# Windowed attention and a feed-forward layer on one core: joining 64-bit weights on VectorE alone, and taking the second chunk's masks and transposes off TensorE

## The chip, the core and the metric

The kernel runs on one core of one Trainium2 chip. The metric is the device time of one launch in microseconds; the median of three runs of the kernel before is 801.97 us (801.61 to 802.2). Engines are named as in the profile: PE is TensorE, DVE is VectorE, ACT is ScalarE, POOL is GpSimd, and SP issues every DMA.

## The reference

```python
def _attn_ref(q, k, v):                       # (8, 8, 576, 64)
    scores = scale * np.matmul(q, k.transpose(0, 1, 3, 2))
    rel = pos[:, None] - pos[None, :]
    mask_plain = (rel >= 0) & (rel < window)                                   # window 32, heads 0 to 3
    mask_dil = (rel >= 0) & (rel < window * dilation) & (rel % dilation == 0)  # dilation 4, heads 4 to 7
    ...
    return np.matmul(attn, v)

def _moe_ref(x, w_in, w_out):                 # x (4608, 512), w_in (512, 2048), w_out (2048, 512)
    h = x @ w_in
    g = 0.5 * h * (1.0 + erf(h * inv_sqrt2))
    return (g @ w_out).astype(np.float32)
```

The attention output, heads side by side, is the `x` of the feed-forward layer. `w_in` and `w_out` arrive as 64-bit floats.

## The kernel before, in words

The 4608 tokens are cut into nine chunks: chunk `c` for `c` below 8 holds the first 512 positions of batch `c`, chunk 8 the last 64 positions of all batches. Chunk 0 goes through the feed-forward layer alone, while the weights are still coming in. The other eight go in four pairs of chunks (`two_chunks`), with a scheme of seven products in place of eight.

All dense products are made of float32r matmuls. Every operand is held as two parts, a rounded high part and the remainder, and a product is three matmuls: high by high, low by high, high by low. Each is one 128x128 weight against 512 columns; there are 3120 of them in the program. L565 is the first layer of chunk 0 (`h_part`, 192 matmuls), L585 its second layer (`ffn_o`, 192), L1108 the first layer of chunks 1 and 2 (384), L1181 and L1296 the layers of the rest.

**Weights.** One of 16 tiles holds 128 columns of `w_in` and 128 rows of `w_out`, 1 MB in 64 bits. `w_load` fetches it as pairs of 32-bit words. Then `w_mid` on ACT shifts the words by 16 bits, `w_split` on DVE takes five steps to build a float32 cut to the high part's bits and the exact remainder, and `w_high` copies the high part as float32r. The first four tiles are done in halves (`HALVED`). `w_away` writes the parts of a tile to a scratch tensor in DRAM, from where later stages fetch them.

**Attention.** A pair `s` is two heads of one chunk; a chunk has four. `scores` makes 32 blocks of 32 queries by 64 keys on PE. For chunks 0 and 1 the mask comes from PE too: two matmuls of 128x256 (L358) put it into PSUM ahead of the scores, which accumulate on it. `lowest` takes row maxima on DVE, `softmax` runs eight exponentials per pair on ACT, `inverse` and `norm` divide. For chunks 0 and 1 `turn_pe` transposes the probabilities on PE (four matmuls per pair, L491) and copies them out of PSUM into `zeros`, a tile in which every second block of 32 columns stays zero, so that `av_early` can contract over all 128 rows at once (16 matmuls per pair, L509). For chunks 2 to 7 the mask is applied by DVE as it reads the scores, `turn` transposes in 32x32 blocks on DVE, `move` lets ACT carry four blocks to other rows (L484), and `av` contracts over 64 rows (32 matmuls per pair, L530 in chunk 2). `xout` leaves `x`, in two parts.

**Order.** Up to the end of chunk 0 the order on every engine is written out by hand: `ORDER` is a string of words that is walked once, and each word runs the next step of one job on one engine. A letter names the job (q, Q, R load queries and keys of chunks 0, 1, 2; v, V values; d loads a weight; k, w, j are `w_mid`, `w_split`, `w_high`; s scores, l lowest, e softmax, i inverse, n norm, t turn, a the product with values, x `xout`, capitals for chunk 1, @ for chunk 2; h, g, o are the first layer, the GELU and the second layer; z is `w_away`), the letter after the colon the engine (p PE, a ACT, v DVE, d DMA). A word such as `*511` puts 11 matmuls of 128x512 without use into PSUM bank 5; there are 25 such matmuls. After that a planner (`Flow`) orders the rest from costs and due times; `duos` holds the times at which it wants the attention of chunks 2 to 8.

Of the kernel before, what the change touches and what calls it, by code (L numbers as in the profile page):

```python
# [39 lines left out]
ORDER = ("q0:d s0:p l0:v d0:d k0:a q1:d *36 s1:p w0:v l0:v w0:v w0:v d1:d k0:a q2:d q3:d w0:v e0:a e0:a j0:a k1:a v1:d w0:v "  # L40
# [111 lines left out]
def attn_ffn(ctx: ExitStack, tc: tile.TileContext, qk, qk_lp, qk_ld, v, v_ld, w, outT):  # L152
# [53 lines left out]
    zeros = wpool.tile([P, 2, 2, 2, 4, 2, KB], F32, tag="w", name="zeros")  # L206
    nc.gpsimd.memset(zeros, 0.0)
# [44 lines left out]
    def w_split(f):  # L252
        for cols in halves(f):
            mid, top, t = raws[f][:, cols, 0], raws[f][:, cols, 1], spare[:, cols]
            yield
            nc.vector.tensor_scalar(t, top, 3, 0x3FFFF000, op0=ALU.logical_shift_left, op1=ALU.bitwise_and)
            yield
            nc.vector.tensor_scalar(mid, mid, 0x01FFFFFF, None, op0=ALU.bitwise_and)
            yield
            nc.vector.scalar_tensor_tensor(top, top, 0xC0000000, t, op0=ALU.bitwise_and, op1=ALU.bitwise_or)  # L260
            yield
            nc.vector.tensor_scalar(t, top, 0xFF800000, None, op0=ALU.bitwise_and)
            yield
            nc.vector.scalar_tensor_tensor(part_of(f, 1, cols), tiled(mid), 2.0 ** -36, tiled(t.bitcast(F32)), op0=ALU.mult, op1=ALU.mult)

    def w_high(f):
        for cols in halves(f):
            e = yield
            copy(e, part_of(f, 0, cols), tiled(raws[f][:, cols, 1].bitcast(F32)))
# [57 lines left out]
    def load_v(s):  # L327

        yield {"DMA": 2.53}
        t = wpool.tile([P, 2, NU, 2, 2 * D], F32, tag="w", name="v_sb")  # L330
        nc.sync.dma_start(t, v[s.c, s.p // 2])
        for i in range(2):
            o = xs[s.c][s.p + i]
            o.v = t[:, i] if s.c > 1 else t[:, i].rearrange("p u j d -> p (u j) d").rearrange("p (a r) d -> p a r d", a=2)
# [10 lines left out]
    def slot(s, u):  # L345
        if s.c < 2:
            return u % 2 * 2 + u // 2
        return u if s.plain or s.rest else (u - 1) % NU

    def scores(s, bank):  # L350
# [5 lines left out]
        if s.c < 2:  # L356
# [4 lines left out]
        for u in range(NU):  # L361
            for r in range(4):
# [6 lines left out]
                for h in range(2):  # L369
# [3 lines left out]
                                     x[:, k0:k0 + s.nk], start=s.c > 1, stop=s.c > 1 or u == NU - 1)  # L373

    def lowest(s):
# [8 lines left out]
        if s.c < 2:  # L384
# [35 lines left out]
    def softmax(s):  # L420
# [6 lines left out]
        for i in range(2 * NU):  # L427
            if i % 4 == 0 and s.c == 0 or i == 0 or s.c > 1:
                yield {"ACT/exp": 1.2 if s.c == 0 else 2.4}
            t = s.sm[i // NU][:, i % NU]  # L430
            at = s.at + i % NU * 2 * KB
            nc.scalar.activation(t, s.sc[:, i // NU, at:at + 2 * KB] if s.c < 2 else t, AF.Exp, bias=s.st[:, 0, i:i + 1],  # L432
                                 scale=SCALE if s.c < 2 else -1.0, accum_out=s.st[:, 1, i:i + 1])
# [52 lines left out]
    def turn_pe(s):  # L486

        yield
        bank = s.bank + (s.p % 2 if s.c else 0)
        for i in range(NU):  # L490
            nc.tensor.transpose(ps[:, bank, i * P:(i + 1) * P], s.all[:, 2 * i:2 * i + 2].rearrange("p i k -> p (i k)"),  # L491
                                diag.bitcast(F32))
        s.t = zeros[:, s.p % 2]
        for k in range(2):
            e = yield
            rows = slice(64 * k, 64 * k + 64)
            copy(e, s.t[rows].rearrange("p h a r k q -> p (h a) r k q")[:, :, :, k],
                 ps[rows, bank].rearrange("p (i r q) -> p i r q", r=4, q=KB))

    def av_early(s):  # L500

        yield
        bank = s.bank + (s.p % 2 if s.c else 1)
        s.px = ps[:, bank]
        x = s.px.rearrange("p (r k a q) -> p a r k q" if s.plain else "p (k a q r) -> p a r k q", k=2, a=2, r=4)
# [953 lines left out]
```

## Time and profile before

| | |
|---|---|
| median of 3 runs | 801.97 us |
| lowest, highest | 801.61, 802.2 us |
| span of the profiled execution | 801.2 us |
| PE busy | 791.7 us (99%) |
| DVE busy | 652.2 us (81%) |
| ACT busy | 532.3 us (66%) |
| DMA moved | 214.62 MB, 268 GB/s on average |

The profiled execution is not one of the three timed runs, so what lies around its span is known from the median alone: 801.97 - 801.2 = 0.8 us. The share of busy time is an average over stages. PE's busy time covers pipelined matmuls whose ends are modelled, so that the distance between the starts of two blocks, and not the busy time, tells what a block costs. The chain of waits (the chain that ended last) shows which engine held the end back at each moment.

### The profile page before, as it was taken

Reading aid. Unit: us, or ns where it says so; the run is one execution under the profiler, and the core shown is the slowest. Engines: PE = TensorE matmul, PEld = TensorE weight load, DVE = VectorE, ACT = ScalarE, POOL = GpSimd, SP = SyncE. Lnnn points to the kernel's source line nnn. Section 1 sums busy time; section 2 is a strip of 40 time slices with the busy share of each in tenths; the row PEclk is TensorE's granted clock in tenths of the full one; section 3 lists DMA queues with packets and bytes.
Section 4 is the critical chain, followed back from the end, with each engine's and each line's share of the span. In section 5 each row is a group of like instructions: output and inputs, shape, how many; then the busy total and the mean of one; then the engine's idle time right before and its main releaser. Section 6 shows DMA issues by size and latency. Waiting matters only on the chain.

```text
span 801.2 us, 19134 instructions
## 1 busy us (share of the span) xinstructions
PE 791.7 (99%) x7806; PEld 650.6 (81%) x7806; DVE 652.2 (81%) x1081; ACT 532.3 (66%) x1294; POOL 39.2 (5%) x63
## 2 busy tenths in 40 slices
PE   7999999999999999999999999999999999999998
PEld 5888888888888878888888888888888888888886
DVE  7999989998999989778897688778986753589753
ACT  8998869678896467786654479775744534565441
POOL 6000033310000000000000000000000000000000
PEclk9999999999999999999999999999999999999999
DMA  9999974999987989674864489558654399555002
GB/s 371 417 415 392 395 272 140 337 353 398 412 307 260 367 317 353 261 301 134 347 244 157 159 317 380 200 210 321 232 211 158 120 388 366 181 205 198 12 1 105
DMA packets 53384, 214.62 MB, mean 268 GB/s; under 512 B 4913, under 2 KB 5425, under 8 KB 36273
## 3 DMA queue, kind: packets, MB, share of 16 engines
q1 hardware_dynamic: 53296, 213.40, 70.3%
q8 instruction: 61, 1.00, 0.5%
q14 instruction: 27, 0.21, 0.1%
HBM read 167.51 MB, written 42.99 MB: 263 GB/s over the span
## 4 chain that ended last, share of the span: by engine, by line
PE 95%; ACT 2%; DMA 1%; DVE 1%; SPq 0%; issue 0%; DVEq 0%; ACTq 0%
PE ps L1296 36%; PE ps L1181 29%; PE ps L1108 11%; PE ps L565 6%; PE ps L585 5%; PE ps L372 3%; PE ps L544 2%; DMA raw_qk<-qk 1%; PE ps L509 1%; ACT sm L432 1%; DVE parts L1039 1%; PE ps L491 1%; PE ps L522 1%; PE ps L530 0%; PE ps L647 0%; ACT turned L484 0%
## 5 line engine op out<-in xcount | busy, mean ns | idle before, releaser
L1296 PE MATMUL ps<-parts,ring 128*128 128x512 f32 x1344 | 308.2, 390 | 0.1
L1296 PEld LDWEIGHTS ps<-parts,ring 128*128 128x128 f32 x1344 | 251.4, 188 | 53.5 <-ACT u L171 0.5
L1181 PE MATMUL ps<-parts,ring 128*128 128x512 f32 x1008 | 232.7, 391 | 0.0
L1181 PEld LDWEIGHTS ps<-parts,ring 128*128 128x128 f32 x1008 | 188.3, 188 | 40.2
L1032 ACT CAST parts<-c 128x512 fp32r<-128x512 f32 x224 | 135.3, 620 | 94.8 <-DVE parts L1039 46.7
L1039 DVE TENSOR_TENSOR parts<-c,parts 128x512 fp32r<-128x512 f32 x224 | 151.7, 687 | 44.5 <-ACT parts L1032 42.4
L1215 DVE TENSOR_TENSOR c<-c 128x512 f32<-128x512 f32 x128 | 84.9, 685 | 0.0
L1165 ACT ACTIVATE c<-c 128x512 f32<-128x512 f32 x96 | 58.9, 629 | 33.8 <-DVE c L1158 30.1
L432 ACT ACTIVATE sm<-sm,st 128x64 f32<-128x64 f32 (+1 forms) x224 | 75.5, 339 | 4.6 <-DVE st L418 4.4
L173 DVE COPY c<-ps 128x512 f32<-128x512 f32 x60 | 41.4, 691 | 41.1 <-PE ps L1181 40.6
L1158 DVE TENSOR_TENSOR c<-c,ps 128x512 f32<-128x512 f32 x72 | 49.3, 686 | 16.2 <-PE ps L1181 13.4
L171 ACT COPY c<-ps 128x512 f32<-128x512 f32 x44 | 25.7, 588 | 41.0 <-PE ps L1181 38.4
L565 PE MATMUL ps<-x,weight 128*128 128x512 f32 x192 | 46.9, 394 | 0.0
L484 ACT COPY turned<-half 32x256 f32<-32x256 f32 x104 | 42.0, 404 | 6.1 <-DVE turned L474 3.5
L585 PE MATMUL ps<-g,weight 128*128 128x512 f32 x192 | 45.7, 390 | 0.0
L1108 PE MATMUL ps<-x,weight 128*128 128x512 f32 x192 | 45.4, 393 | 0.0
L1108 PE MATMUL ps<-x,ring 128*128 128x512 f32 x192 | 44.9, 392 | 0.0
L432 ACT ACTIVATION_READ_ACCUMULATOR sm<-sm,st 128x1 f32 x224 | 42.1, 188 | 0.0
L1108 PEld LDWEIGHTS ps<-x,ring 128*128 128x128 f32 x192 | 35.7, 188 | 7.7
L585 PEld LDWEIGHTS ps<-g,weight 128*128 128x128 f32 x192 | 35.9, 188 | 7.5
L1108 PEld LDWEIGHTS ps<-x,weight 128*128 128x128 f32 x192 | 35.6, 188 | 7.7
L565 PEld LDWEIGHTS ps<-x,weight 128*128 128x128 f32 x192 | 35.5, 188 | 7.6
(104 smaller groups left out, 778.3 us busy)
## 6 DMA issues: line engine op xcount, KB each, us to landing
ring<-sums SPq DMA_DIRECT2D x56, 1024.0 KB, 6.9
ring<-plain SPq DMA_DIRECT2D x46, 1024.0 KB, 8.4
v_sb<-v SPq DMA_DIRECT2D x17, 1024.0 KB, 12.0
raw_qk<-qk SPq DMA_DIRECT2D x32, 512.0 KB, 10.2
raw_w<-w SPq DMA_DIRECT2D x16, 1024.0 KB, 16.1
plain<-weight SPq DMA_DIRECT2D x32, 512.0 KB, 11.3
sums<-units SPq DMA_DIRECT2D x16, 1024.0 KB, 10.5
units<-plain SPq DMA_DIRECT2D x4, 1024.0 KB, 11.1
```

The lines of the kernel that those rows point to most:

```text
L432: nc.scalar.activation(t, s.sc[:, i // NU, at:at + 2 * KB] if s.c < 2 else t, AF.Exp, bias=s.st[:, 0, i:i + 1], scale=SCALE if s.c < 2 els ...
L484: nc.scalar.copy(s.t[32 * to:32 * to + 32, r % 2], s.half[32 * r:32 * r + 32])
L565: nc.tensor.matmul(bank, column(weights[f], t, cc), x[:, xx], start=n == 0, stop=n == 3 * NC - 1)
L585: nc.tensor.matmul(ps[:, d], column(weights[f], t, NC + d), gs[f][:, u], start=first and n == 0, stop=last and n == 2)
L1032: nc.scalar.copy(to if len(x.shape) == 2 else to.rearrange("p (g i) -> p g i", i=32), x)
L1039: nc.vector.tensor_sub(a, x, b)
L1108: nc.tensor.matmul(bank, column(w, i, cc), x[:, j], start=k == 0, stop=k == 3 * NC - 1)
L1158: nc.vector.tensor_add(C[f][:, part], C[f][:, part], ps[:, bank_of(bank)])
L1165: nc.scalar.activation(C[f][:, part], C[f][:, part], AF.Gelu)
L1181: nc.tensor.matmul(ps[:, bank_of(bank)], w()[:, a, i * P:(i + 1) * P], made[n, u, i][:, b], start=begins and k == 0, stop=k == 5, skip_gro ...
L1215: op(C[f][:, to], C[f][:, a], C[f][:, b])
L1296: nc.tensor.matmul(ps[:, bank_of((n, b, d))], w()[:, i, d * P:(d + 1) * P], made[key][:, j], start=begins and f == 0 and k == 0, stop=f == ...
```

## The change

`w_mid` and `w_split` go, and `w_whole` takes their place: three steps on DVE build a whole float32 from the two words. `w_high` copies it as float32r on ACT (or DVE) as before, and the new `w_low` subtracts that copy from it on DVE. In the attention of chunk 0 the tile with zero halves goes: `turn_pe` copies the four transposes out in one piece into `facing`, and `av_early` contracts over 64 rows, in twice as many matmuls of half the columns. Chunk 1 is treated as chunks 2 to 7 are: mask in DVE's pass, `turn` on DVE, `move` on ACT, `av` on PE. The first layer's first four tiles get four PSUM banks, so that all four can be under way at once. `ORDER` is written anew, with 12 matmuls without use instead of 25, and `duos` has new times.

```diff
-ORDER = ("q0:d s0:p l0:v d0:d k0:a q1:d *36 s1:p w0:v l0:v w0:v w0:v d1:d k0:a q2:d q3:d w0:v e0:a e0:a j0:a k1:a v1:d w0:v "
+ORDER = ("q0:d s0:p l0:v l0:v e0:a e0:a d0:d w0:v w0:v w0:v w0:v j0:a q1:d *25 s1:p l1:v l1:a e1:a e1:a w0:v i0:v k0:v i0:v "
...
-    zeros = wpool.tile([P, 2, 2, 2, 4, 2, KB], F32, tag="w", name="zeros")
-    nc.gpsimd.memset(zeros, 0.0)
+    facing = wpool.tile([P, NPAIR, 2, 2, 4, KB], F32, tag="w", name="facing")
...
-    def w_mid(f):
-
-        for cols in halves(f):
-            yield
-            raw = raws[f][:, cols].bitcast(U16).rearrange("p n t -> p (n t)").rearrange("p (n t) -> p n t", t=4)
-            nc.scalar.copy(raw[:, :, 0:2], raw[:, :, 1:3])
...
-    def w_split(f):
+    def w_whole(f):
         for cols in halves(f):
-            mid, top, t = raws[f][:, cols, 0], raws[f][:, cols, 1], spare[:, cols]
+            low, top, t = raws[f][:, cols, 0], raws[f][:, cols, 1], spare[:, cols]
             yield
-            nc.vector.tensor_scalar(t, top, 3, 0x3FFFF000, op0=ALU.logical_shift_left, op1=ALU.bitwise_and)
+            nc.vector.tensor_scalar(t, top, 3, 0x3FFFFFF8, op0=ALU.logical_shift_left, op1=ALU.bitwise_and)
             yield
-            nc.vector.tensor_scalar(mid, mid, 0x01FFFFFF, None, op0=ALU.bitwise_and)
+            nc.vector.scalar_tensor_tensor(t, low, 29, t, op0=ALU.logical_shift_right, op1=ALU.bitwise_or)
             yield
             nc.vector.scalar_tensor_tensor(top, top, 0xC0000000, t, op0=ALU.bitwise_and, op1=ALU.bitwise_or)
-            yield
-            nc.vector.tensor_scalar(t, top, 0xFF800000, None, op0=ALU.bitwise_and)
-            yield
-            nc.vector.scalar_tensor_tensor(part_of(f, 1, cols), tiled(mid), 2.0 ** -36, tiled(t.bitcast(F32)), op0=ALU.mult, op1=ALU.mult)
...
+    def w_low(f):
+        for cols in halves(f):
+            yield
+            nc.vector.tensor_sub(part_of(f, 1, cols), whole_of(f, cols), part_of(f, 0, cols))
...
     def scores(s, bank):
-        if s.c < 2:
+        if s.c == 0:
...
     def turn_pe(s):
-        s.t = zeros[:, s.p % 2]
-        for k in range(2):
-            e = yield
-            rows = slice(64 * k, 64 * k + 64)
-            copy(e, s.t[rows].rearrange("p h a r k q -> p (h a) r k q")[:, :, :, k],
-                 ps[rows, bank].rearrange("p (i r q) -> p i r q", r=4, q=KB))
+        s.t = facing[:, s.p]
+        e = yield
+        copy(e, s.t.rearrange("p h a r q -> p (h a r q)"), ps[:, s.bank])
...
     def av_early(s):
-                for h in range(2):
-                    nc.tensor.matmul(x[h * D:(h + 1) * D, a, r], s.v[:, a, r, h * D:(h + 1) * D],
-                                     s.t[:, h, a, r].rearrange("p k q -> p (k q)"), start=True, stop=True)
+                for k in range(2):
+                    rows = slice(64 * k, 64 * k + 64)
+                    for h in range(2):
+                        nc.tensor.matmul(x[h * D:(h + 1) * D, k, a, r], s.v[rows, a, r, h * D:(h + 1) * D],
+                                         s.t[rows, h, a, r], start=True, stop=True)
...
+    def hidden_bank(f):
+        return ps[:, (4, 5, 0, 1)[f] if f < 4 else 4 + f % 2]
...
-        return dict(l=lowest, e=softmax, i=inverse, n=norm, t=turn_pe, a=av_early)[kind](s)
+        return dict(l=lowest, e=softmax, i=inverse, n=norm, t=turn if s.c else turn_pe, m=moved, a=av_early)[kind](s)
...
-    duos = [(2, 0, 0.1, (0, 0), 9.8), (2, 2, 1.5, (3.0, 5.0), 15.9),
+    duos = [(2, 0, -5.9, (0.0, 0.0), 11.8),
+            (2, 2, -3.3, (0.2, 2.2), 13.1),
```

The functions `scores`, `lowest`, `softmax` and `xout` test `s.c == 0` where they tested `s.c < 2`, and the host lays out the values of chunk 1 as it does those of chunks 2 to 7.

How the instructions move, on PE at the start of the program. `early` holds the masks, `sm` the probabilities, `x,weight` is the first layer of chunk 0, `g,weight` its second layer. Before:

```order
L491 MATMUL ps<-early,sm 128x128 x4
L647 MATMUL ps<-early 128x512 x11
L491 MATMUL ps<-early,sm 128x128 x4
L509 MATMUL ps<-zeros,v_sb 64x2x32 x16
L647 MATMUL ps<-early 128x512 x2
L491 MATMUL ps<-early,sm 128x128 x4
L509 MATMUL ps<-zeros,v_sb 64x2x32 x16
L491 MATMUL ps<-early,sm 128x128 x4
L509 MATMUL ps<-zeros,v_sb 64x2x32 x16
L565 MATMUL ps<-x,weight 128x512 x6
L509 MATMUL ps<-zeros,v_sb 64x2x32 x16
L565 MATMUL ps<-x,weight 128x512 x18
```

The same place with the change:

```order
L486 MATMUL ps<-early,sm 128x128 x4
L653 MATMUL ps<-early 128x512 x7
L486 MATMUL ps<-early,sm 128x128 x4
L504 MATMUL ps<-facing,v_sb 64x32 x64
L564 MATMUL ps<-x,weight 128x512 x9
L486 MATMUL ps<-early,sm 128x128 x4
L564 MATMUL ps<-x,weight 128x512 x3
L486 MATMUL ps<-early,sm 128x128 x4
L504 MATMUL ps<-facing,v_sb 64x32 x64
L564 MATMUL ps<-x,weight 128x512 x36
```

Twelve matmuls of the first layer now stand ahead of the last two products with values, where six stood, and fewer matmuls without use stand between the transposes.

The same stretch on DVE with the change, from the first weight's remainder to the second pair's probabilities (L248, L250, L252 are `w_whole`, L265 `w_low`, L439 the reciprocal, L453 `norm`, L382 the row maxima):

```order
L265 TENSOR_TENSOR weight<-raw_w,weight 128x2x256
L439 RECIPROCAL st<-st 128x8
L382 TENSOR_REDUCE st<-ps 128x8
L453 TENSOR_TENSOR sm<-sm,st 128x512
L248 TENSOR_SCALAR spare<-raw_w 128x512
L250 SCALAR_TENSOR_TENSOR spare<-raw_w,spare 128x512
L252 SCALAR_TENSOR_TENSOR raw_w<-raw_w,spare 128x512
L248 TENSOR_SCALAR spare<-raw_w 128x512
L439 RECIPROCAL st<-st 128x8
L250 SCALAR_TENSOR_TENSOR spare<-raw_w,spare 128x512
L453 TENSOR_TENSOR sm<-sm,st 128x512
```

The second weight tile's first steps now stand ahead of the second pair's `norm`; that weight is the sixth transfer that SP issues, as the fourth pair's queries and keys were before.

ACT ahead of the second half of chunk 1's products with values (L571, L574 are the GELU and its rounding, L428 the exponentials, L480 `move`, L451 a `norm` on ACT, L550 `xout`):

```order
L480 COPY turned<-half 32x256 x4
L571 ACTIVATE gf<-ps 128x512
L451 ACTIVATE sm<-sm,st 128x64 x8
L574 CAST g<-gf 128x512
L571 ACTIVATE gf<-ps 128x512
L428 ACT_TABLE_LOAD
L428 ACTIVATE sm,st<-sm,st 128x64 x4
L480 COPY turned<-half 32x256 x4
L550 CAST x<-ps 128x512 x2
L428 ACTIVATE sm,st<-sm,st 128x64 x7
L574 CAST g<-gf 128x512
L571 ACT_TABLE_LOAD
L571 ACTIVATE gf<-ps 128x512
L480 COPY turned<-half 32x256 x4
```

The moves of chunk 1's blocks, which did not exist, stand in one queue with the GELUs of chunk 0 and the exponentials of chunk 2.

## Rows read from the trace of the kernel before

**Rows 1.** The page: busy time of PE and the other engines; shares of the chain.

```profile
PE 791.7 (99%) x7806; PEld 650.6 (81%) x7806; DVE 652.2 (81%) x1081; ACT 532.3 (66%) x1294; POOL 39.2 (5%) x63
...
PE 95%; ACT 2%; DMA 1%; DVE 1%; SPq 0%; issue 0%; DVEq 0%; ACTq 0%
```

**Rows 2.** Chain of waits, start and end: start us, us, what.

```profile
3.16 11.29 DMA raw_qk<-qk
...
25.14 1.58 PE ps L565 x6
26.72 1.08 PE ps L509 x32
27.80 4.30 PE ps L565 x18
...
797.41 0.02 issue
```

**Rows 3.** Chain of waits, pieces of chunk 1 and chunk 2 on PE.

```profile
32.11 0.23 PE ps L358 x2
32.34 0.79 PE ps L372 x53
...
34.35 2.95 PE ps L565 x12
37.30 2.72 PE ps L585 x12
...
61.79 0.87 PE ps L491 x8
...
65.40 2.02 PE ps L509 x64
...
129.30 1.41 PE ps L372 x91
130.71 8.41 PE ps L1108 x36
139.12 2.00 PE ps L530 x128
```

**Rows 4.** Groups on PE over the run, shapes apart: busy, mean ns | idle before.

```profile
L544 PE MATMUL ps<-v_sb,turned 64*32 64x64 f32 x1408 | 16.8, 225 | 0.1
```

**Rows 5.** Timeline of DVE, 21 to 24 us: start, duration, instruction.

```profile
21.68 0.20 DVE L443 RECIPROCAL st<-st 128x8 f32<-128x8 f32 x1
21.92 0.69 DVE L457 TENSOR_TENSOR sm<-sm,st 128x512 f32<-128x512 f32 x1
...
23.25 0.42 DVE L256 TENSOR_SCALAR spare<-raw_w 128x512 uint32<-128x512 uint32 x1
...
23.91 0.69 DVE L260 SCALAR_TENSOR_TENSOR raw_w<-raw_w,spare 128x512 uint32<-128x512 uint32 x1
```

**Rows 6.** Timeline of ACT: `xout` reading PSUM.

```profile
22.02 0.59 ACT L554 CAST x<-ps 128x512 fp32r<-128x512 f32 x1
```

**Rows 7.** Groups on ACT over the run: `move` and `w_mid`.

```profile
L484 ACT COPY turned<-half 32x256 f32<-32x256 f32 x104 | 42.0, 404 | 6.1 <-DVE turned L474 3.5 <-DVE st L441 0.8
...
L236 ACT COPY raw_w<-raw_w 128x2048 uint16<-128x2048 uint16 x12 | 23.0, 1931 | 0.0
```

**Rows 8.** Windows: length, busy time (x instructions) by engine, PEclk, DMA share, GB/s.

```profile
10.00:20.00 10.00, 7.63 (x154) 6.24 (x152) 9.90 (x25) 9.52 (x46) 5.29 (x16) 0.83 1.02 418
20.00:126.58 106.58, 106.58 (x1061) 88.17 (x1060) 99.16 (x153) 91.81 (x195) 11.56 (x9) 1.00 0.92 356
```

**Rows 9.** Chain of waits, `turn` of a pair of chunk 3 on DVE.

```profile
246.71 0.45 DVE half L471
247.16 0.60 DVE turned L474
```

**Rows 10.** Timeline of PE, first 16 us: matmuls without use, last scores of chunk 0.

```profile
5.41 2.57 PE L647 MATMUL ps<-early 128*128 128x512 f32 x6
...
14.49 1.26 PE L372 MATMUL ps<-raw_qk 64*32 64x64 f32 x64 [1.33 <-DMA raw_qk<-qk]
```

More of the change, by code (lines that the diff above doesn't have):

```diff
@@ L355, in scores @@
         s.sc = ps[:, bank:bank + 2]
-        if s.c < 2:
+        if s.c == 0:
             for h in range(2):
@@ L372, in scores @@
                     nc.tensor.matmul(s.sc[32 * r:32 * r + 32, h, c0:c0 + s.nk], x[:, q0:q0 + 32],
-                                     x[:, k0:k0 + s.nk], start=s.c > 1, stop=s.c > 1 or u == NU - 1)
+                                     x[:, k0:k0 + s.nk], start=s.c > 0, stop=s.c > 0 or u == NU - 1)
     def lowest(s):
@@ L383, in lowest @@
         n = NU * s.nk
-        if s.c < 2:
+        if s.c == 0:
             yield {"DVE": 0.7}
@@ L427, in softmax @@
         for i in range(2 * NU):
-            if i % 4 == 0 and s.c == 0 or i == 0 or s.c > 1:
-                yield {"ACT/exp": 1.2 if s.c == 0 else 2.4}
+            if i % 4 == 0 or s.c > 1:
+                yield {"ACT/exp": 1.2}
             t = s.sm[i // NU][:, i % NU]
             at = s.at + i % NU * 2 * KB
-            nc.scalar.activation(t, s.sc[:, i // NU, at:at + 2 * KB] if s.c < 2 else t, AF.Exp, bias=s.st[:, 0, i:i + 1],
-                                 scale=SCALE if s.c < 2 else -1.0, accum_out=s.st[:, 1, i:i + 1])
+            nc.scalar.activation(t, s.sc[:, i // NU, at:at + 2 * KB] if s.c == 0 else t, AF.Exp, bias=s.st[:, 0, i:i + 1],
+                                 scale=-1.0 if s.c else SCALE, accum_out=s.st[:, 1, i:i + 1])
     def inverse(s):
@@ L488, in turn_pe @@
         yield
[L489 removed]
         for i in range(NU):
[L491 removed]
+            nc.tensor.transpose(ps[:, s.bank, i * P:(i + 1) * P], s.all[:, 2 * i:2 * i + 2].rearrange("p i k -> p (i k)"),
                                 diag.bitcast(F32))
[L493 to L498 removed]
+        s.t = facing[:, s.p]
+        e = yield
+        copy(e, s.t.rearrange("p h a r q -> p (h a r q)"), ps[:, s.bank])
     def av_early(s):
         yield
[L503 to L505 removed]
+        s.px = ps[:, s.bank:s.bank + 2, 0:256]
+        x = s.px.rearrange("p k (r a q) -> p k a r q" if s.plain else "p k (a q r) -> p k a r q", a=2, r=4)
         for a in range(2):
             for r in range(4):
[L508 to L510 removed]
+                for k in range(2):
[3 more added lines that the diff above has]
+                                         s.t[rows, h, a, r], start=True, stop=True)
     def av(s, px, u0=0):
@@ L549, in xout @@
         s.x = xg.tile([P, 2, N], F32R, tag="xg", name="x")
-        if s.c < 2:
-            put = (s.px, s.x[:, 0], s.x[:, 1])
+        if s.c == 0:
+            at = "p (r k i) -> p k r i" if s.plain else "p (k r i) -> p k r i"
+            put = (s.px.rearrange("p k (r i) -> p k r i", r=4),) + tuple(s.x[:, t].rearrange(at, k=2, r=4) for t in range(2))
         else:
@@ L556, in xout @@
         nc.vector.tensor_sub(put[2], put[0], put[1])
+    def hidden_bank(f):
+        return ps[:, (4, 5, 0, 1)[f] if f < 4 else 4 + f % 2]
     def h_part(f, ccs):
         yield
-        bank = ps[:, 4 + f % 2]
+        bank = hidden_bank(f)
         n = 3 * ccs[0]
@@ L571, in hidden_of @@
         gf = work.tile([P, N], F32, tag="go", name="gf", bufs=GO)
-        nc.scalar.activation(gf, ps[:, 4 + f % 2], AF.Gelu)
+        nc.scalar.activation(gf, hidden_bank(f), AF.Gelu)
         yield
@@ L593, in store, with views @@
         nc.sync.dma_start(outT[d * P:(d + 1) * P, c * N:(c + 1) * N], o)
+    def views(s):
+        c0 = s.p % 2 * 256
+        s.both = ps[:, 6:8, c0:c0 + 256].rearrange("p k (j i) -> p k j i", j=2)
+        return lambda r: ps[:, 6 + r // 2, c0 + r % 2 * P:c0 + r % 2 * P + P]
     xs = {c: [new_pair(c, p) for p in range(NPAIR)] for c in range(NCH)}
@@ L617, in job @@
         if kind in "kwj":
-            return dict(k=w_mid, w=w_split, j=w_high)[kind](int(i))
+            return dict(k=w_low, w=w_whole, j=w_high)[kind](int(i))
         if kind == "h":
@@ L631, in job @@
             return together([scores(xs[1][p], 6) for p in (2 * int(i), 2 * int(i) + 1)])
+        if kind == "A":
+            return together([av(s, views(s)) for s in xs[1][2 * int(i):2 * int(i) + 2]])
         s = xs[int(kind.isupper())][int(i)]
@@ L636, in job @@
         if kind == "x":
-            return xout(s, None)
-        return dict(l=lowest, e=softmax, i=inverse, n=norm, t=turn_pe, a=av_early)[kind](s)
+            return xout(s, s.c and s.both)
+        return dict(l=lowest, e=softmax, i=inverse, n=norm, t=turn if s.c else turn_pe, m=moved, a=av_early)[kind](s)
     begun = {}
@@ L970, in attend @@
                 vs = [flow.add("DMA", 2.6, load_values(s), due=values_at - 6, begin=values_at - lead[1], take=[("w", key)], land=2.3)]
-            for o in pairs:
-                def view(r, o=o):
-                    c0 = o.p % 2 * 256 + r % 2 * P
-                    return ps[:, 6 + r // 2, c0:c0 + P]
-                o.view = view
-                o.px = ps[:, 6:8, o.p % 2 * 256:o.p % 2 * 256 + 256].rearrange("p k (j i) -> p k j i", j=2)
-            visit = flow.add("PE", 2.05 if c == 2 else ROWS, pe_work([av(s, s.view), av(t, t.view)] if c == 2 else [av_rows(pairs)]),
+            visit = flow.add("PE", 2.05 if c == 2 else ROWS, pe_work([av(s, views(s)), av(t, views(t))] if c == 2 else [av_rows(pairs)]),
                              turned + vs, take=[("upper", up)], give=[key] + [("turned", c, o.p, 0) for o in pairs])
@@ L983, in attend @@
                 for o in pairs:
-                    go = stepper(xout(o, o.px))
+                    go = stepper(xout(o, o.both))
                     j = flow.add("ACT", 0.65, go, [visit], values_at + 2, take=[("xg", ("xc", c, o.p))])
@@ L1430 @@
     v_all = np.concatenate([vs, rest[None]], 0)
-    for c in range(2):
-        one = vc[c].reshape(NPAIR, 2, 4, 2, 2, 2 * KB, D).transpose(0, 3, 5, 4, 2, 1, 6)
-        v_all[c] = one.reshape(NPAIR, P, NU, 2, 2 * D)
+    one = vc[0].reshape(NPAIR, 2, 4, 2, 2, 2 * KB, D).transpose(0, 3, 5, 4, 2, 1, 6)
+    v_all[0] = one.reshape(NPAIR, P, NU, 2, 2 * D)
     v_all = v_all.reshape(NCH, 2, 2, P, NU, 2, 2 * D).transpose(0, 1, 3, 2, 4, 5, 6)
```

12 lines of the change are left out of this document (5 added, 7 removed), and 47 rows, old and new, of tables (ORDER, duos).

## The prediction, made before the changed kernel ran

> **What bounds the kernel now.** I read the page first: PE is busy 99% of the span and carries 95% of the chain that ended last [rows 1]. Busy time alone is not proof, because the ends of matmuls are modelled, so I went on to the chain in order of time. Its first long piece is a transfer: the queries and keys of the last pair of chunk 0 land at 3.16 + 11.29 = 14.45 us. The first useful dense matmuls start at 25.14, the last product with values of chunk 0 ends at 27.80, and PE's last matmul ends at 797.41 [rows 2]. In between twelve dense matmuls take 2.72 us wherever one looks, 0.2267 us each [rows 3], and PE's small matmuls there show almost no idle time (0.1 us in all before L544) [rows 4]. So from 25 us on, the end is a sum: what PE has to do, plus what it waits. The reader should take two things from this. Work taken off PE after 25 us comes off the end one for one, as long as DVE and ACT keep up. And before 25 us the end moves only if the dense stream starts earlier, or if less small work is left inside it.
>
> The other engines are close behind in this stage: from 20 us to chunk 0's end at 126.58 us DVE is busy for 99.16 of 106.58 us and ACT for 91.81, with the DMA engines at 0.92 [rows 8]. That is where the risk lies.
>
> The threshold for a visible difference is 0.2% of 801.97, 1.6 us. I make the sum against the profiled span, 801.2, and carry the 0.8 us around it unchanged, so I subtract from the median.
>
> **Chunk 1's masks: -1.7 us.** A mask and its scores for two pairs stand at 32.11 to 34.35, 2.24 us. The same scores without masks in chunk 2 take 1.41. The difference, 0.83, falls away twice [rows 3]. The mask now rides on a pass of DVE that must read the scores anyway; what is new there is the separate pass for the row minima.
>
> **Chunk 1's transposes: -1.7 us.** Eight on PE cost 0.87 us [rows 3], twice.
>
> **Products with values: 0.** Half the rows and half the columns in twice as many matmuls looks like a trade. The rows say it is none: the old form takes 2.02 us for two pairs, the new form, which chunk 2 already uses, 2.00 [rows 3]. I take 0 for chunk 1 and the same 2.00 for each half of chunk 0. The form itself is in the trace, so the price has no wide bounds; between L509 and L530 they are 0 and -0.04 per two pairs.
>
> The Trainium skill speaks against this edit: "TensorE: Matmul & The Clock Gate", section "Wait — 56ns, not 53.3ns?", says that matmuls never start less than about 25 ns apart however few columns they have. By that, the 128 recorded matmuls of a visit would take 3.2 us, each visit of chunk 1 would cost 1.2 us more, and the whole change would come to about -1.1 us. The trace disagrees: 128 in 2.00 us is 15.6 ns [rows 3], so the sum goes by the row.
>
> **The start: -1.3 us.** The sixth transfer on the queue decides, as before. It is now the second weight (1 MB) behind 3 MB of others; before it was a half-megabyte load behind 3.5 MB. The bytes up to its end are the same, 4 MB, so I let it land at 14.45 again [rows 2]. DVE then does three steps of that weight, a fourth, a reciprocal, a fifth and `norm` of the second pair: 0.42 + 0.69 + 0.69 + 0.42 + 0.20 + 0.69 + 0.69 = 3.8 us by full durations [rows 5]; independent ones overlap a little, so `norm` ends at about 18.0. Then four transposes (half of 0.87) and the first product with values (half of 2.00) on PE, `xout` on ACT (0.59, [rows 6]) and the remainder on DVE (0.69): 20.7, with four hand-overs of 0.1 21.1. From there PE does 9 dense matmuls (2.04), transposes (0.44), 3 dense (0.68), transposes (0.44) and the last two products (2.00), 5.6 us, plus about 0.6 for the changes between shapes (18 dense matmuls after small ones take 4.30 in place of 4.08, [rows 2]) and 0.5 that I allow for the last two pairs' `norm`: 27.8. At that moment chunk 0's attention is through and 12 dense matmuls are done; before, at 27.80, it was 6. Six matmuls are 1.36 us, less a little: -1.3. The bounds: without the waits and hand-overs -2.2; with a slow clock as in the first rival, +1.8. The 13 matmuls without use that go stood in waiting time and count nothing by themselves.
>
> **Weights on DVE: 0, hidden.** Per half tile, DVE had three short steps and two long ones, 3 x 0.42 + 2 x 0.69 = 2.64 us; now one short and three long, 2.49 [rows 5]. Over 32 halves that frees 4.8 us. Chunk 1 takes it back: a further pass for each of four pairs (2.8), two transposes per pair (0.45 + 0.60 each, 4.2, [rows 9]), less five copies out of PSUM (3.4). DVE ends about even. ACT loses `w_mid`, 1.93 us for each of twelve whole tiles and about half that for each of the eight half tiles of the first four [rows 7], 31 us in all; it gains sixteen moves of 0.40, 6.5 us. What covers all this is PE's dense stream; if DVE fell behind, that cover would be gone (second rival).
>
> **New waits: +1.2 us.** The moves stand in ACT's queue between the GELUs that feed the second layer and the exponentials of chunk 2, and PE's visit needs the last of them. Bounds: 0, since the same arrangement in chunks 3 to 7 cost PE 0.1 us [rows 4]; 3.2, if all eight moves of one visit (8 x 0.404, [rows 7]) come when PE is there. I take three moves, 1.2, nearer to the lower row, but not at it, because this stage is tighter than the later ones [rows 8]. Behind a waiting visit stand the dense matmuls of the second layer, so such a wait reaches the end.
>
> **Chunks 2 to 8: 0.** Their work is unchanged; new times shift when it runs. PE's idle time there was almost nothing [rows 4], so there is nothing to gain, and half a microsecond to lose.
>
> Sum: -1.7 - 1.7 - 1.3 + 1.2 = -3.5, from 801.97 to **798.5 us**.
>
> **Rivals.**
>
> *The clock falls at the start.* In 10 to 20 us the granted clock averaged 0.83 of full [rows 8]: PE had waited for transfers, and the scores at 14.49 then took 1.26 us where full speed takes 0.79 [rows 10, 3]. With 13 fewer matmuls without use, and PE waiting for `norm` up to 18 us, the lower level (1.2 GHz) could last through the first dense ones. A dense matmul at that level takes 2.57 / 6 = 0.43 [rows 10], so twelve cost 2.4 more, and the first two products, by 1.26 against 0.79, 1.2 more; the 0.5 of waits would be hidden. Start +1.8 in place of -1.3, total -0.4: 801.6, no visible change. The Trainium skill, same page, Part 1, has the lower level as the default that activity releases; by that rule the trace agrees in the first 8 us, and no run here yet shows how the new order fares. For it: the fewer fillers. Against: the transposes, fillers and products still keep PE at work most of the time.
>
> *DVE is the bound.* It was busy for 93% of the stage [rows 8], and PE would now reach every weight 3 to 4 us sooner. If the weights come no sooner, the 3.4 us of masks and transposes turn into waits for weights, and only the start remains: -1.3, 800.7, no visible change. For it: the 93%. Against: freed and added work balance, and the new work comes late in the stage, behind most of the weights.
>
> *ACT is late for chunk 1 (slower).* If the queue ahead of the moves runs so late that all sixteen reach PE's visits uncovered, PE waits 6.5 us in place of 1.2: -4.7 + 6.5 = +1.8, 803.8. It turns measurably slower from 6.3 us of waiting. For it: the moves, exponentials and GELUs of three chunks in one queue. Against: ACT sheds 25 us on balance.
>
> *The floor of 25 ns holds* for these matmuls after all: 800.9, no visible change.
>
> **How the numbers follow.** Forecast 0.75; clock 0.08; DVE 0.06; floor 0.03; ACT late 0.08. Faster by over 0.2% is the forecast, 0.75; within 0.2% the three middle cases, 0.17; slower 0.08. The range reaches down to the start's better bound without new waits, -2.2 - 3.4 = -5.6, 796.4, and up to the clock's case, 801.6; left out are ACT late and some tails.
>
> **What would show it.** In the changed profile: first dense matmuls near 21 us; the last product with values of chunk 0 ending near 28 with 12 dense ones done; two scores of chunk 1 at 1.4 us; no L491-like transposes after 26; products with values at 2.0 us; chunk 2's first layer starting about 3.5 us sooner than 126.58; PE waiting about 1 us on ACT or DVE before it. The prediction is wrong if the granted clock stays below full after 18 us, if PE waits for weights for more than 2 us in 30 to 120, or if the gain at the start of chunk 2's first layer is lost later.

## The result, and the profile after

The changed kernel takes **808.52 us** (median; 807.52 to 808.95) against 801.84 (median of four runs, one more than before): a ratio of 1.0082, 95% interval 1.0068 to 1.0096. It is slower by 6.7 us, where 798.5 us was forecast. The profiled execution is the fastest of the four, 807.52 us, its span 805.7 us.

The page: PE's busy time fell by 3.8 us against [rows 1], of which some 2.5 us are the matmuls without use that went (25 took 8.3 us, 12 take 5.8); its share of the chain fell from 95% to 82%.

```profile
PE 787.9 (98%) x8025; PEld 646.4 (80%) x8025; DVE 648.0 (80%) x1053; ACT 526.9 (65%) x1321; POOL 35.1 (4%) x62
...
q8 instruction: 63, 1.03, 0.5%
...
PE 82%; DVE 6%; DMA 6%; ACT 4%; issue 2%; SPq 1%; DVEq 0%; ACTq 0%
```

What PE waited for over the run (us in total, times, longest; `issue` stands where the profile shows no cause):

```profile
PE ps L368 <- DMA raw_qk<-qk: 6.4, 1, 6.4
PE ps L368 <- issue: 3.0, 1, 3.0
...
PE ps L525 <- ACT turned L480: 0.8, 1, 0.8
```

Where these stand, from PE's timeline (start, duration, instructions, idle time before and its releaser):

```profile
14.09 1.06 PE L368 MATMUL ps<-raw_qk 64*32 64x64 f32 x52 [2.99 <-issue]
...
15.85 3.33 PE L653 MATMUL ps<-early 128*128 128x512 f32 x7
18.98 0.79 PE L486 MATMUL ps<-early,sm 128*128 128x128 f32 x4
...
22.33 2.34 PE L564 MATMUL ps<-x,weight 128*128 128x512 f32 x9 [0.57 <-DVE x L552]
...
28.21 8.50 PE L564 MATMUL ps<-x,weight 128*128 128x512 f32 x36
...
54.59 1.48 PE L368 MATMUL ps<-raw_qk 64*32 64x64 f32 x128
...
112.92 2.16 PE L525 MATMUL ps<-turned,v_sb 64*64 64x32 f32 x128 [0.82 <-ACT turned L480]
...
123.30 2.88 PE L1108 MATMUL ps<-x,weight 128*128 128x512 f32 x12
...
132.57 2.05 PE L368 MATMUL ps<-raw_qk 64*32 64x64 f32 x128 [6.39 <-DMA raw_qk<-qk]
134.55 7.69 PE L1108 MATMUL ps<-x,weight 128*128 128x512 f32 x31
```

Read it from the top. Chunk 0 is through at 28.21 with 12 dense matmuls done, and chunk 1's scores stand without masks. Counted by dense matmuls, PE leads the kernel before by 3.1 us when chunk 2's first layer begins at 123.30 (before: 126.41 on the same timeline). Then PE stops for 6.39 us at the scores of chunk 2's second two pairs, because queries and keys of one of them have not landed. The lead of 3.1 becomes a lag of 4.3 within 25 dense matmuls around this stop (the 375th to the 400th), and the lag is 4.5 at PE's last matmul. So one place decides. (The lag is 4.5 us between two profiled executions and 6.7 us between the medians: that of the changed kernel was 1.0 us faster than its median, and that of the kernel before some 1.2 us slower than its own, as the section on the prediction works out.)

The load that PE waits for is `R2`, the queries and keys of chunk 2's third pair. The chain of waits has it (start, us): issued at 120.89, landed 11.63 us later, at 132.5.

```profile
120.89 11.63 DMA raw_qk<-qk
```

The new `ORDER` has it last of all transfers, behind sixteen write-backs (`z`). And the queue ahead of it was late. What SP waited for on behalf of the write-backs from 20 to 215 us, before:

```profile
SPq L290 <- DVE weight L264: 12.0, 3, 4.4
```

and after:

```profile
SPq L286 <- DVE weight L265: 37.1, 4, 17.7
```

SP's timeline after the change shows the longest of these. Weight 5's write-back is next in line after 29.37 and can be issued only at 48.36, when DVE has made its second part; four loads stand behind it:

```profile
29.37 0.33 SPq L222 DMA_DIRECT2D raw_w<-w  x1
48.36 0.90 SPq L286 DMA_DIRECT2D plain<-weight  x2
49.31 3.12 SPq L222 DMA_DIRECT2D raw_w<-w  x4
...
120.89 0.54 SPq L321 DMA_DIRECT2D raw_qk<-qk  x1
```

The windows say what that costs (the last three columns are PEclk, DMA share, GB/s). Before:

```profile
40.00:50.00 10.00, 10.00 (x46) 8.29 (x45) 9.86 (x14) 9.03 (x9) 0.00 (x0) 1.00 1.02 424
...
80.00:90.00 10.00, 10.00 (x46) 8.29 (x45) 9.93 (x14) 7.31 (x18) 0.00 (x0) 1.00 1.05 382
```

After, with the start and the stretch of the wait, in both of which the granted clock falls too:

```profile
10.00:20.00 10.00, 7.01 (x135) 5.50 (x132) 8.10 (x18) 6.09 (x37) 3.54 (x10) 0.66 1.01 417
...
40.00:50.00 10.00, 10.00 (x128) 8.32 (x112) 9.87 (x13) 4.65 (x10) 0.00 (x0) 1.00 0.47 189
...
80.00:90.00 10.00, 10.00 (x167) 8.17 (x166) 10.00 (x13) 9.88 (x35) 0.00 (x0) 1.00 0.66 218
...
130.00:140.00 10.00, 7.43 (x150) 6.38 (x151) 5.24 (x9) 2.00 (x3) 3.51 (x2) 0.73 1.00 387
```

### The profile page after: what moved, and what is told of

It reads as the page before. It is cut to its first block, busy times and chain, and to the rows that moved or that the text cites. A ratio compares the mean times of both kernels' runs of the same rounds, so it can differ in the third digit from the quotient of the medians.

```text
span 805.7 us, 19562 instructions
## 1 busy us (share of the span) xinstructions
PE 787.9 (98%) x8025; PEld 646.4 (80%) x8025; DVE 648.0 (80%) x1053; ACT 526.9 (65%) x1321; POOL 35.1 (4%) x62
## 3 DMA queue, kind: packets, MB, share of 16 engines
q8 instruction: 63, 1.03, 0.5%
## 4 chain that ended last, share of the span: by engine, by line
PE 82%; DVE 6%; DMA 6%; ACT 4%; issue 2%; SPq 1%; DVEq 0%; ACTq 0%
PE ps L1296 34%; PE ps L1181 29%; PE ps L1108 7%; DMA plain<-weight 3%; PE ps L368 3%; PE ps L564 3%; DMA raw_qk<-qk 2%; PE ps L584 2%; PE ps L539 2%; DVE parts L1039 1%; ACT sm L428 1%; DVE c L1215 1%; PE ps L653 1%; ACT turned L480 1%; DVE units L819 1%
## 5 line engine op out<-in xcount | busy, mean ns | idle before, releaser
L428 ACT ACTIVATE sm<-sm,st 128x64 f32<-128x64 f32 (+1 forms) x256 | 86.2, 338 | 0.9 <-DVE st L414 0.6
L480 ACT COPY turned<-half 32x256 f32<-32x256 f32 x120 | 48.4, 404 | 2.7 <-DVE turned L470 0.6
L428 ACT ACTIVATION_READ_ACCUMULATOR sm<-sm,st 128x1 f32 x256 | 48.0, 188 | 0.0
## 6 DMA issues: line engine op xcount, KB each, us to landing
raw_w<-w SPq DMA_DIRECT2D x16, 1024.0 KB, 12.2
```

The lines of the kernel that those rows point to most:

```text
L480: nc.scalar.copy(s.t[32 * to:32 * to + 32, r % 2], s.half[32 * r:32 * r + 32])
```

## Experiments: the late load

*The load moved forward in the changed kernel, and moved to the end in the kernel before.*

```diff
-h14:p R3:d z9:d z7:d
+h14:p R3:d R2:d z9:d z7:d
...
-z12:d z4:d R2:d @m0:a
+z12:d z4:d @m0:a
```

> The changed kernel with one move: chunk 2's last queries and keys (the second half of raw_qk) are loaded right behind the other duo's, ahead of eleven write-backs and the fetch of the next chunk, instead of behind all of them. Theory A, the load stood last in a late queue: the 6.39 us wait of TensorE at line 368 near 126 us goes, and with it the half clock behind it; the matmuls behind it lose nothing against the ones ahead (7.4 us were lost between dense matmul 375 and 400), so 808.5 - 7.4 = 801.1 us, 800.3 to 802. Theory B, the queue itself is too slow, whatever its order: the write-backs pushed back make another transfer late, a wait of 3 to 6 us shows at a weight or a chunk, and the time stays at 804 to 809 us. Theory C, the start (the 2.99 us in which TensorE had no instructions, and the half clock behind it) is what the end keeps: no change, 808.5 us.

> The kernel before with one move: the load of chunk 2's last queries and keys goes to the end of the order of transfers, behind all write-backs, as the change has it. Theory A, last place only hurts where the queue is late: here the last write-back landed at 117.4 us, so the load lands near 120 to 122 us, before TensorE wants it, and the time stays at 801.8 us (801.2 to 802.5). Rival, last place alone costs the time: a wait at line 368 of 3 us or more, 804.5 us or more.

Measured: 802.08 us (ratio 1.0004, 0.9994 to 1.0014) and 802.33 us (1.0003, 0.9994 to 1.0012). The early load takes the whole loss away, 6.4 us; last place by itself costs nothing where the queue is on time (in the kernel before, the load moved to the end was issued at 113.31, and PE came to its scores at 129.38). Both halves of theory A hold, except that 801.1 was expected: a further 1 us is lost later. PE's timeline with the early load:

```profile
126.12 1.48 PE L369 MATMUL ps<-raw_qk 64*32 64x64 f32 x128
127.53 11.18 PE L1109 MATMUL ps<-x,weight 128*128 128x512 f32 x48
...
192.95 0.85 PE L369 MATMUL ps<-raw_qk 64*32 64x64 f32 x64 [0.82 <-DVE turned L471]
194.11 0.86 PE L369 MATMUL ps<-raw_qk 64*32 64x64 f32 x64 [0.31 <-DMA raw_qk<-qk]
...
209.07 7.23 PE L1109 MATMUL ps<-x,ring 128*128 128x512 f32 x31 [0.68 <-issue]
```

The dense matmuls behind the scores start 7.02 us sooner (127.53 against 134.55): 6.39 of waiting, and 0.6 because the scores after the wait ran at the lower of the two clock levels (2.05 against 1.48).

*One write-back moved behind four loads; then all sixteen put in the order of their weights, as they had been before.*

```diff
-w7:v d8:d z5:d d9:d d10:d d11:d d12:d w7:v
+w7:v d8:d d9:d d10:d d11:d d12:d z5:d w7:v
```

> The changed kernel with one move: the write-back of weight 5, which waits some 19 us at the head of the queue for its converted half while the DMA engines go idle (about 45.6 to 50.9 us), is issued behind the loads of weights 9 to 12 instead of ahead of them. Theory A1, a write that waits at the queue's head is what makes the queue late: the 5 us of idle transfers come back, chunk 2's last load lands 3 to 5 us sooner than 132.5 us, and the time falls to 803.5 to 805.5 us. Rival A2, the lateness is bound later (the 12 us that another write-back waits near 71 to 83 us, or the rate of the mixed reads and writes): the load still lands near 132 us, and the time stays at 808.5 us (807.5 to 809).

Of the order of transfers, the `z` words alone:

```diff
-z5 z6 z1 z11 z3 z9 z7 z10 z8 z13 z0 z15 z2 z14 z12 z4
+z0 z1 z2 z3 z4 z5 z6 z7 z8 z9 z10 z11 z12 z13 z14 z15
```

> The changed kernel with one thing undone: the sixteen write-backs stand in the order of their weights (0 to 15), as before the change, at the same sixteen places; the load of chunk 2's last queries and keys stays behind all of them. Theory F, the queue is late because a write-back of a weight that DVE has not joined yet waits at its head (37.1 us in four waits, the longest 17.7, against 12.0 in three before): with weights that are ready the idle stretches of the DMA engines at 45 to 51 and 70 to 90 us fill, the load lands 5 to 9 us sooner than 132.5 us, and the time falls to 801 to 804 us. Rival G, reads and writes together simply take until then: the load lands near 132 us and the time stays at 808.5 us (807.5 to 809).

Measured: 808.92 us (1.0083, 1.0068 to 1.0098) and 802.93 us (1.001, 1.0001 to 1.0019). Moving one write-back only moves the idle stretch (DMA share 1.01 in 40 to 50 us, but 0.59 and 0.60 in 70 to 90): the next write-backs are not ready either. So theory A1 falls and A2 holds. With all in order, the load, still last, is issued at 114.42 in place of 120.89, and the wait is gone. SP's wait for DVE's weights on behalf of write-backs (L287) fell from 37.1 to 3.8 us; more of it than before is on loads (L223):

```profile
SPq L223 <- DVE weight L266: 14.4, 2, 12.2
...
SPq L287 <- DVE weight L266: 3.8, 2, 2.2
```

and the first idle window is full again, while the second is not:

```profile
40.00:50.00 10.00, 10.00 (x103) 8.29 (x89) 9.86 (x12) 4.87 (x11) 0.00 (x0) 1.00 1.03 392
...
80.00:90.00 10.00, 10.00 (x166) 8.15 (x165) 10.00 (x14) 9.88 (x36) 0.00 (x0) 1.00 0.63 191
```

Theory F expected both to fill. In the second, SP now waits for DVE on behalf of a load, 12.2 us; of the 6.5 us by which `R2` is issued sooner, the first window alone makes up 5.6 (10 us at a share of 1.03 in place of 0.47).

So the cause of the result is settled from two sides: undoing either the place of the load or the order of the write-backs brings the time back to that of the kernel before. The kernel before with both of them was not tried.

## Experiment: the start

*Chunk 0's fourth scores behind the first transposes.*

```diff
-q3:d s3:p n0:v t0:p d1:d
+q3:d n0:v t0:p s3:p d1:d
```

> The changed kernel with one move: on TensorE, chunk 0's fourth score tile (52 of its 128 matmuls came after the 2.99 us gap) stands behind the first group of transposes instead of ahead of it, where the others' instructions may by then have come. Theory A, the late load sets everything behind 126 us: whatever the start gains is waited off there, and the time stays at 808.5 us (807.8 to 809.2), with a longer wait at line 368. Theory C, the start is what the end keeps: 1 to 3 us less, 805.5 to 807.5 us. If the gap is only moved (the instructions come no sooner) the first dense matmul stays at 22.3 us under both.

Measured: 808.52 us (1.0082, 1.0066 to 1.0097), with the wait at line 369 grown to 6.8 us. The first dense matmul starts at 22.28 in place of 22.33, so the start came no sooner, and by itself this run does not decide on theory C: the gap at the scores is gone, but PE waits 2.4 us for `norm` and 0.9 us without a named cause instead, and with a granted clock of 0.83 in 20 to 30 us the first nine dense matmuls take 3.54 us in place of 2.34. Theory C falls by the early load, which keeps a gap of 2.54 us and the first dense matmul at 22.32 and gets the whole loss back.

## Experiments: where the lead of 3.1 us goes

*Old due times for chunks 3 to 8 (`duos`), with the early load; then the same with TensorE's later instructions shifted by 66 places; then the shift with the early load alone.* The rows of chunks 5 to 8 are left out of the first diff. For the shift a new word, `~36`, runs 36 matmuls of 32x64 without use, and three of the seven long ones go: 33 matmuls more, each with its weight load.

```diff
-            (3, 0, 27.2, (25.9, 31.9), 41.7, (9, 10)),
...
-            (4, 0, 56.8, (60.7, 65.9), 83.8, (9, 12)),
-            (4, 2, 81.5, (83.0, 85.0), 103.2, (9, 12)),
...
+            (3, 0, 21.2, (25.9, 31.9), 41.7, (9, 10)), (3, 2, 35.7, (45.9, 47.9), 63.3, (9, 10)),
+            (4, 0, 62.8, (66.7, 71.9), 91.2, (9, 12)), (4, 2, 81.5, (83.0, 85.0), 101.5, (9, 12))]
...
```

> The changed kernel with chunk 2's last queries and keys loaded early (802.1 us) and the planner's due times for the attention of chunks 3 to 8 as before the change. Up to dense matmul 500 (156 us) nothing should differ. Theory D, the new due times cost what was still lost there: TensorE waited 0.82 us for the turned tile of DVE, 0.31 us for queries and keys and 0.68 us for something the profile does not name between 192 and 210 us, as it was sent to chunk 3's scores 36 dense matmuls sooner than before; with the old times these go, the lead of 3.1 us over the kernel before stays to the end, and the time is 799 to 800.5 us. Rival E, the queue is late, not the order: such waits come back in other places, and the time stays at 801.5 to 803 us.

```diff
-n1:v *57 t1:p
+n1:v *54 ~36 t1:p
```

> The early load with the old due times (812.7 us), and 33 matmuls without use more in the stretch before 20 us in which TensorE waits anyway (3 of the 7 long ones go, 36 of 32x64 come), so that every later TensorE instruction stands 66 places further on in its stream. Theory H, TensorE ran out of instructions there: its fetches are 256 instructions each, and in both waits in chunk 8's products (2.41 and 3.23 us, near 579 and 595 us) it stopped after the same 193rd instruction of a block, at a visit that needs 384 instructions in 2 us; shifted by 66 the block ends elsewhere, the two waits and the half clock behind them go, and the time falls by 6 to 10 us to 802 to 806 us. Rival D2, the old due times make the visits themselves wait (for a transfer or another engine that the profile does not name): both waits stay, 811 to 814 us.

> The early load alone (802.1 us) with the same 33 matmuls more before 20 us. Theory H: the 0.68 us without a named cause at 209 us and the visit of 2.02 in place of 1.48 us at 179 us are ends of instruction blocks too; they move, and the time changes by up to 1.5 us either way, 800.5 to 803.5 us, while the waits for DVE (0.82) and for queries and keys (0.31) stay. Rival: the waits at 179 and 209 us are data, so nothing moves: 801.6 to 802.6 us with the same two rows.

Measured: 812.72 us (1.0131, 1.0116 to 1.0146), 805.1 us (1.0031, 1.0021 to 1.004) and 810.88 us (1.0114, 1.0099 to 1.0129). (The scores between 192 and 195 us, which the expectation counts to chunk 3, are chunk 4's first.) Theory D falls, and so does the range of theory E (801.5 to 803): with the old times the lead at 561 us is 1.1 us, with the new ones 1.0, and then 10 us are lost at chunk 8's products, 5.6 of them to waits that no other engine releases, and the rest behind these, where the granted clock was 0.88 (570 to 600 us):

```profile
576.74 1.73 PE L518 MATMUL ps<-turned,v_wide 32*64 32x32 f32 x153
580.88 0.65 PE L518 MATMUL ps<-turned,v_wide 32*64 32x32 f32 x39 [2.41 <-issue]
...
592.84 1.95 PE L518 MATMUL ps<-turned,v_wide 32*64 32x32 f32 x173
598.01 0.63 PE L518 MATMUL ps<-turned,v_wide 32*64 32x32 f32 x19 [3.23 <-issue]
```

A shift of 66 instructions, put where PE waits anyway, removes both. Of the 3.0 us that are left above the early load alone, a new wait of 2.6 us near 30 us, which both shifted kernels have, is the largest part. In the early load's kernel the same shift costs 8.8 us; its two new waits are

```profile
32.81 3.36 PE L565 MATMUL ps<-x,weight 128*128 128x512 f32 x14 [2.62 <-issue]
...
212.32 0.58 PE L540 MATMUL ps<-v_sb,turned 64*32 64x64 f32 x18 [4.26 <-issue]
```

Theory H holds, and its size was underrated (up to 1.5 us expected in the last run). A count settles it. In all traces of the changed kernel and of what was made of it, PE's waits of over 0.2 us without a named cause, 32 with those in the first 20 us, come at seven places only: behind 445, 698, 1209, 4788, 5809, 13692 or 14201 recorded instructions of TensorE, weight loads included. These lie whole multiples of some 255 apart, and the shifted kernels have their waits at the same places, where other matmuls now stand: the wait of 4.26 us comes where the unshifted kernel has the one of 0.68. The waits for DVE and for queries and keys stayed, as expected; so did the product of 2.02 us, which therefore has another cause.

*Early load and ordered write-backs together; all three; and with GpSimd's additions held back.*

> Early load and write-backs in the order of their weights together, due times of the change. If the late queue is also what costs the rest (theory E), the DMA engines have free time before 200 us and the waits there go: 799.5 to 801 us. If the new due times do (theory D), nothing changes against the early load alone: 801.5 to 802.7 us.

> All three: early load, write-backs in the order of their weights, due times of before. Theories D and E both say that at least the lead of 3.1 us at chunk 2's first layer now reaches the end: 798.5 to 800 us, below both kernels. If it comes out at 801.5 us or more, the lead is lost by something that neither names.

```diff
-    nc.gpsimd.tensor_copy(gate, weights[NF - 1][0:1, 3, 1, 0:8].bitcast(F32))
+    nc.gpsimd.tensor_copy(gate, gs[NF - 1][0:1, 1, 0:8].bitcast(F32))
```

> Early load and write-backs in the order of their weights (802.9 us), and GpSimd's additions for the later stages wait for the last second part of the hidden layer instead of for the last weight. Theory P, GpSimd slows DVE: from 108 to 120 us GpSimd now ran without a gap, and DVE's subtraction of two tensors took 1206 ns on average in place of 870, so TensorE waited 1.5 us at the second layer near 116 us; with GpSimd held back the wait goes, the lead at chunk 2's first layer is 3.0 us again instead of 1.5, and the time is 800.5 to 802 us. Rival, the second part is late for another reason: the 1.5 us stay, 802.5 to 803.5 us.

Measured: 802.91 us (1.001, 1.0001 to 1.0019), 814.39 us (1.0145, 1.0115 to 1.0174) and **800.54 us (0.9984, 0.9974 to 0.9993)**. All three together missed, for the reason above: chunk 8's waits came back (5.4 us). Early load and ordered write-backs gained nothing together and miss the ranges of both theories, because a new wait of 1.5 us had come in at 116 us, PE for DVE's second part of the hidden layer. With ordered write-backs GpSimd no longer waits for them, and its additions run through that stretch:

```profile
108.08 11.79 POOL L808 TENSOR_TENSOR units<-weight 128x512 f32<-128x512 f32 x8
```

DVE's groups in 100 to 122 us, with the write-backs in order (and the load last):

```profile
L577 DVE TENSOR_TENSOR g<-gf,g 128x512 fp32r<-128x512 f32 x4 | 4.7, 1206 | 0.0
L553 DVE TENSOR_TENSOR x<-ps,x 128x512 fp32r<-128x512 f32 x4 | 3.3, 848 | 0.0
```

and with GpSimd starting only at 117.85:

```profile
L553 DVE TENSOR_TENSOR x<-ps,x 128x512 fp32r<-128x512 f32 x4 | 3.4, 866 | 0.2 <-ACT x L551 0.2
L577 DVE TENSOR_TENSOR g<-gf,g 128x512 fp32r<-128x512 f32 x4 | 2.7, 670 | 1.3 <-ACT g L575 1.3
```

The subtraction of two SBUF tiles goes back from 1206 to 670 ns; the one that reads PSUM does not change. These means mix instructions beside GpSimd with others. DVE's timeline with the write-backs in order, where GpSimd's additions end at 119.87, keeps them apart:

```profile
108.02 0.65 DVE L553 TENSOR_TENSOR x<-ps,x 128x512 fp32r<-128x512 f32 x1
...
112.06 0.64 DVE L553 TENSOR_TENSOR x<-ps,x 128x512 fp32r<-128x512 f32 x1
...
115.26 3.45 DVE L577 TENSOR_TENSOR g<-gf,g 128x512 fp32r<-128x512 f32 x2
...
120.18 0.64 DVE L577 TENSOR_TENSOR g<-gf,g 128x512 fp32r<-128x512 f32 x1
```

Beside GpSimd two subtractions of SBUF tiles take 3.45 us, some 1.7 each; alone one takes 0.64. The wait is gone, theory P holds, and this version beats both kernels, if only by 0.16% against the one before. Its lead is 3.1 us at chunk 2's first layer, 2.1 after dense matmul 700 and 2.8 at PE's last matmul. Whether holding GpSimd back would also help without the other two edits was not tried.

To this version, the old due times of chunks 3 and 4 alone (the rows of the diff above):

> The version with early load, write-backs in the order of their weights and GpSimd held back (800.5 us), and the due times of chunks 3 and 4 alone as before the change, so that chunk 3's scores come 12 dense matmuls later again. With the queue repaired the profile shows no wait at these scores any more, so theory E says that the times matter no more: 800.0 to 801.0 us. Theory D would have 799.0 to 800.0 us, as the lead of 3.1 us at chunk 2's first layer shrinks to 2.1 us by 210 us. Theory H allows either a gain or a loss of some us, since the visits meet other ends of TensorE's instruction blocks between 190 and 265 us; a wait without a named cause there would show it.

Measured: 801.91 us (0.9998, 0.9989 to 1.0007), 1.4 us more. Theory D falls again, and E's range (800.0 to 801.0) is missed too; a loss with a wait of no named cause is what H allowed. PE's timeline shows two waits in the products of chunk 3, one on ACT's moves and one without a named cause:

```profile
180.03 1.63 PE L540 MATMUL ps<-v_sb,turned 64*32 64x64 f32 x116 [0.54 <-ACT turned L481]
...
210.44 0.32 PE L540 MATMUL ps<-v_sb,turned 64*32 64x64 f32 x9 [1.11 <-issue]
```

## Why the prediction was wrong, point by point

**The step that failed** is "Chunks 2 to 8: 0", with its reason, "Their work is unchanged; new times shift when it runs." What moved there is not work but transfers. The sum went through PE, DVE and ACT; the DMA queue was followed at the start alone, and behind it the share of 0.92 [rows 8] was named as a risk and given no price. The new `ORDER` showed both moves, `R2` to the end and the write-backs out of order, and neither got a term. The missing term is +7.4 us in the profile: 6.39 of waiting and 1.0 for the lower clock behind it.

- *Chunk 1's masks, -1.7; transposes, -1.7; products, 0*: right. Scores take 1.48 on the timeline and 1.41 on the chain, products 2.07 and 2.0 as in [rows 3], and the last transposes start at 25.64 us.
- *The start, -1.3*: nearly right, -1.0 (the thirteenth dense matmul starts at 28.21, before at 29.23). The last product of chunk 0 ended at 28.21 (27.8 worked out), with 12 dense matmuls done as said. The first dense matmul came at 22.33 (21.1). `norm` of the second pair ended at 17.77, as worked out (18.0); but the transposes behind it started at 18.98 only, because PE still had the seven matmuls without use ahead of them, which came late behind the gap of 2.99 us and took 3.33 us at the lower clock. So those that stayed did not stand in waiting time alone.
- *New waits on ACT's moves, +1.2*: the mechanism is right, 0.82 us at one visit.
- *Sum up to chunk 2's first layer*: -3.5 forecast, -3.1 measured. Up to 123 us the forecast held.
- *Weights on DVE, hidden*: right for PE, wrong for SP. PE's list of waits has none for a weight, but a queue that stands in order waited 37.1 us for them, because a write-back was asked for before its weight was joined.
- *Chunks 2 to 8, "half a microsecond to lose"*: too small even without the late load. With the early load the lead shrinks from 3.1 to 0.4 at dense matmul 700 (212 us). That it is 1.0 at the end is due to the profiled execution of the kernel before: the same kernel with the load last also gains 0.6 us on it between dense matmuls 700 and 2500.
- *The rivals*: none was this one. The clock did fall at the start, as the first rival has it, to a granted 0.66 in 10 to 20 us (0.83 before, [rows 8]), but it was full again from 20 us on, ahead of the first dense matmul. ACT late (803.8) is the nearest in time, by another mechanism. The floor of 25 ns is refuted once more: 128 matmuls of chunk 1's products in 2.07 us are 16.2 ns each.
- *The signs of being wrong*: the third, the gain lost later, came true. "PE waits for weights" did not; PE waited for queries and keys instead, on the same queue. The first came true for a moment: the granted clock was 0.66 in 18 to 20 us.
- The sum was made against a span of 801.2 with 0.8 us around it. Later profiles show 1.8 us around it (802.01 against 800.2 with the early load), so the profiled execution of before was about 1.2 us longer than its median. The forecast is a difference and does not move by it, but a lead read between two profiles does: with the early load it is 1.0 us at the end, while the medians are the same (802.08 and 802.14).
- What the late load does not explain: the early load alone is still 3.6 us above the forecast, and the best version (800.54) 2.0. Of the 3.6, 0.4 were missing at chunk 2's first layer already, and 2.7 are lost by dense matmul 700.

What stays open: of the 2.7 us of lead lost between dense matmuls 500 (159 us) and 700, 0.82 (DVE), 0.31 (transfer) and 0.68 us (instructions) are named in the early load's trace, and 0.54 of a product is shown to wait on ACT only in the last run; the remaining 0.4 are not traced.

## What to carry to other kernels

Price every transfer that a new order moves: what stands ahead of it in its queue, what those wait for, and when its reader needs it. A write queued before its data are made holds up all loads behind it, so issue writes in the order in which their data become ready, and put a load that the bottleneck engine needs ahead of writes that nobody waits for. A trace with idle DMA engines while transfers are queued is the sign.

## What the runs showed of the hardware

**TensorE can run out of instructions.** In the page of the changed kernel the instruction queue q8 moves 63 blocks, 1.03 MB, 16 KB each, for 16050 instructions of PE and its weight loads: some 255 in a block (61 for 15612 before). Visits of small matmuls use up 256 to 384 instructions in 1.4 to 2 us, and where a block ends in such a visit or soon behind it, PE can stop until the next one has come: 2.41 and 3.23 us in chunk 8, 4.26 us in chunk 3. The traces have the blocks themselves: in the wait of 4.26 us PE stands still from 208.06 to 212.32, and the block moves from 209.92 to 210.81. In all 32 waits PE goes on 1.3 to 1.6 us after the block has moved. The same kernel with 66 instructions more ahead took 8.8 us longer, another 7.6 us less. The Trainium skill, "Runtime: NRT & Kernel Launch", section "Instruction fetch mechanics", has the blocks of 256 instructions, and the traces agree; it also says that fetching is hidden behind the rate of issue, and these waits say that it is not.

**GpSimd slows DVE, and only some of its instructions**: a subtraction with two SBUF inputs takes some 1.7 us beside GpSimd's additions and 0.64 alone, one with an input in PSUM 0.64 and 0.65 beside them. The Trainium skill, "SBUF — State Buffer", section "SBUF: two separate sides", has a DVE instruction with two SBUF inputs and a GpSimd instruction that reads SBUF shut each other out; the trace agrees in which of DVE's instructions slow down. Whether one of the two waits for the whole of the other, no run here shows.
